# A fused attention and two-mixer kernel on one core: exponentials turned in two by rows for every head pair, and a new instruction order

## The chip, the core and the metric

The kernel runs on one core of a Trainium2 chip. The metric is device time in microseconds (us), the median of three runs. The core's engines work from queues of their own: TensorE (PE in the profile, with PEld for its weight loads), VectorE (DVE), ScalarE (ACT), GpSimd (POOL) and SyncE (SP), which issues most of the transfers.

## What is computed

Three stages one after the other, for batch 4, sequence 448, model width 768:

```python
q_n, k_n = rmsnorm(q, g_q), rmsnorm(k, g_k)            # 12 heads of 64
attn = softmax(scale * q_n @ k_n.T)
x = (attn @ v) put together to [4, 448, 768]
h = relu(x @ w_in); u, v = halves of h                  # "moe", widths 512 and 512
v_n = (v - mean(v)) / sqrt(var(v) + 1e-6)
x = (u * (w_spatial @ v_n + b_spatial)) @ w_out
u = x + (relu(x.T @ w_tok1) @ w_tok2).T                 # "moe2"
out = u + relu(u @ w_ch1) @ w_ch2
```

## The kernel before

**Head pairs.** Attention runs over 24 pairs of heads (`NP`), six for each batch item. A pair's queries are cut into four chunks `c` of T = 112 rows. For a pair, `load` fetches raw q and k, `norms` and `scale` divide the rows by their root mean square (for the first pair `first` does it), and `transposed` turns q and k on TensorE into `qt` and `kt` (called `whole` in the profile for the first eight pairs, `WHOLE = 8`). For each chunk `scores` makes the two heads' 112x448 scores in two PSUM banks, VectorE takes the negated row maximum `nm`, ScalarE writes `e`, the exponentials, and sums them. `turned` turns `e` on TensorE into `et`, in seven blocks of 128 columns, by way of PSUM tiles `tp`; ScalarE or VectorE copies these to SBUF. `values` multiplies `et` by v into `av`, VectorE divides by the sums (`over`), and the result goes on as `xp`.

**Two ways to turn.** For pairs under `HALVED = 8` a chunk is turned by seven transposes of all 112 rows. From pair 8 on each of the seven is done as two, of rows 0 to 63 and of rows 64 to 111, with their own PSUM tiles, issued as one joined group. The copies out of PSUM then take 448 and 336 columns, as they do in the other way.

**Weights and the mixers.** While the pairs run, `prepare_v`, `prepare_uo` and `prepare_next` fetch the mixers' weights, convert them (ScalarE takes the absolute value of a word, VectorE does four integer steps, ScalarE rounds the high part, GpSimd subtracts for the low part; tiles `word`, `wv`, `wpart`) and write some of them back to DRAM. `moe` runs for a batch item once its six pairs are done: `vps`, a normalisation over tokens whose root is made by `rsqrt` (ScalarE Ln and Exp, then Newton steps), `ups`, `sps`, `xps`. After the attention come `h1ps` and `u_ps`, and then two products in Strassen form, `h2ps` and `o_ps`.

**Order.** Nothing is issued as it is written down. Every operation is put into a `Plan` with an estimated cost and its dependencies. `issue` runs a list scheduler (`place`) back and forth, then shifts the weights by a list of random seeds (`NUDGES`), places once more, and emits every engine's queue in the order of the planned starts. So one list sets the order of all engines and of the transfers. `warmers` puts matmuls without a use into planned idle times of TensorE longer than `IDLE` = 1500 ns: one for each `PACE` ns, on the first PSUM bank by number that is free in the gap.

All operations are recorded through one helper, so nearly all rows have line 464, the emitting line of `issue`; the useless matmuls have line 456. Rows are told apart by their tiles.

Of the kernel before, what the change touches and what calls it, by code (L numbers as in the profile page):

```python
# [15 lines left out]
AF = mybir.ActivationFunctionType  # L16
# [136 lines left out]
class Plan:  # L153
# [8 lines left out]
    def add(self, engine, fn, args, kwargs):  # L162
# [6 lines left out]
        if out is None:  # L169
# [6 lines left out]
        op.port = engine == "gpsimd" and bool(sbuf) or engine == "vector" and (  # L176
            len(sbuf) > 1 and free(sbuf[1].shape) > 1
            or len(ins) == len(sbuf) and fn in ("tensor_scalar", "tensor_copy"))

# [208 lines left out]
    def warmers(self, start, bank, closes):  # L388


        ops = self.ops
        busy = {}
        for t, n in bank.items():
            us = [i for i, ts in closes.items() if t in ts]
            first = min(start[i] for i in us)
            last = max(start[i] + ops[i].cost + ops[i].late for i in us) + TO["tensor"]
            busy.setdefault(n, []).append((first, last))
        order = sorted((i for i, op in enumerate(ops) if op.engine == "tensor"), key=lambda i: (start[i], i))
        found = {}
        for a, b in zip(order, order[1:]):  # L400
            end = start[a] + ops[a].cost
            idle = start[b] - end
            if idle < IDLE or end < 10000:
                continue
            for n in range(Banks.ALL):
                if all(last <= end or first >= start[b] for first, last in busy.get(n, ())):
                    break
            else:
                continue
            found[b] = [n] * int((idle - SPARE) / PACE)  # L410
        return found
# [59 lines left out]
SWITCH, NEAR, FAR, EARLY = 300, 2500, 10000, 95000  # L471
NUDGED = 4000
NUDGES = (
# [21 lines left out]
)  # L495
ENGINES = "gpsimd", "scalar", "sync", "tensor", "vector"
IDLE, SPARE, PACE = 1500, 200, 275
SHARED = {"vector": "gpsimd", "gpsimd": "vector"}
# [17 lines left out]
def nudged(weight, seed, engines):  # L516


    h = mixed(seed)
    g = mixed(h)  # L520
    at, reach, size = h % NUDGED, (20, 60, 150, 400)[g & 3], (150, 500, 1500, 4000)[g >> 2 & 3]
    way, who = g >> 4 & 3, ENGINES[(g >> 6) % 5]
    weight = list(weight)
    for i in range(max(0, at - reach), min(len(weight), at + reach)):
        if way in (0, 3) or engines[i] == who:
            u = mixed(seed * 2654435761 + (0 if way & 1 else i) & 0xFFFFFFFF)
            weight[i] += size * ((u >> 8) / 8388608.0 - 1.0)
    return weight
# [33 lines left out]
def attention_moe_mixer(  # L562
# [155 lines left out]
    class Attention:  # L718
# [75 lines left out]
        def first(self):  # L794
# [6 lines left out]
            def squares(a, on):  # L801
                sq = p.tile([T, 2, S], F32, tag="e", bufs=EB, name="e").rearrange("p r s -> p (r s)")
                sq = sq[:, :n * D].rearrange("p (n d) -> p n d", d=D)
                if on is nc.scalar:
                    on.activation(sq, raw[:, a], AF.Square)
                else:
                    on.tensor_tensor(sq, raw[:, a], raw[:, a], op=ALU.mult)
                return sq

            def root(a, on, sq, behind=(), copied=()):  # L810
                ss = p.tile([P, n], F32, tag=f"ss{a}", bufs=1, name="ss")
                ss.tile.after = list(behind)
                nc.vector.reduce_sum(ss[:T], sq, axis=AX.X)
                self.r[0][a] = rsqrt(p, ss[:T], T, n, 1.0 / D, f"r{a}", bufs=1, on=on, wait=copied)
# [21 lines left out]
        def scale(self, i):  # L836
# [4 lines left out]
            if i >= WHOLE:  # L841
# [5 lines left out]
                return  # L847
            for a in range(2) if i else (1,):
                on = nc.gpsimd if i > 1 else nc.vector
# [4 lines left out]
        def transposed(self, i, a, wait=()):  # L854
# [13 lines left out]
            t.tile.after = list(t.tile.after) + list(wait)  # L868
            nc.scalar.activation(t, tpf, AF.Copy, scale=1.0 if a == 0 else self.gg[:, 0:1])
            if a:  # L870
# [138 lines left out]
        def start(self):  # L1009
# [5 lines left out]
            self.gg = self.p.tile([P, 1], F32, tag="gg", bufs=1, name="gg")  # L1015
            nc.vector.tensor_tensor(self.gg, g[:, 0:1], g[:, 1:2], op=ALU.mult)
            nc.vector.tensor_scalar(self.gg, self.gg, float(D) ** -0.5, None, ALU.mult)

# [38 lines left out]
    G = S // R  # L1057
    HALVED = 8
    HALVES = (0, R), (R, T - R)
# [158 lines left out]
    def moe(mp, b):  # L1218
# [20 lines left out]
        for t, m in TOK:  # L1239
# [18 lines left out]
            nc.vector.bn_aggr(mv, bs)  # L1258
            r = rsqrt(mp, mv[:, 1:2], P, 1, 1.0, "lr")
            nc.vector.tensor_scalar(vr, vr, mv[:, 0:1], r, ALU.subtract, ALU.mult)  # L1260
# [416 lines left out]
```

## Time and profile before

| | |
|---|---|
| Median of 3 runs | 848.29 us (847.06 to 849.16) |
| The profiled execution, its own time | 851.01 us |
| Its span, first to last instruction | 849.1 us |
| TensorE busy | 837.8 us (99%) |
| VectorE, ScalarE, GpSimd busy | 675.6 (80%), 527.2 (62%), 344.3 us (41%) |
| Chain of work that ended last | PE 85%, ACT 5%, DMA 4%, DVE 4% |
| Mean granted TensorE clock | 0.996 |

Busy times are sums of records. Matmuls are pipelined, so the record of one overlaps the next: the time that a group takes on TensorE is read from its start to the start of the next group, not from its length. PEclk is the granted clock, 1.00 for 2.4 GHz and 0.50 for 1.2 GHz.

### The profile page before, as it was taken

To read this page: it belongs to the slowest core of one execution; us is meant where nothing else is said; L and a number is where in the kernel's file an instruction comes from. 1 tells how busy PE (TensorE), PEld (TensorE's weight loads), DVE (VectorE), ACT (ScalarE), POOL (GpSimd) and SP (SyncE) were. 2 spreads that over 40 slices of the span, in tenths; PEclk is the share of its full clock that TensorE was granted. 3 is DMA by queue.
4 is the path that set the end of the run, shared out by engine and by line. 5 is a ranking of instruction groups with operands and counts; after the bars stand their busy time and mean duration, and the time that the engine had idled before them with its cause. 6 is when DMAs were issued, how large, how long until landed. Compare 5 with 4: busy or idle time off the path is not lost.

```text
span 849.1 us, 16503 instructions
## 1 busy us (share of the span) xinstructions
PE 837.8 (99%) x5538; PEld 704.6 (83%) x5538; DVE 675.6 (80%) x1340; ACT 527.2 (62%) x1268; POOL 344.3 (41%) x431
## 2 busy tenths in 40 slices
PE   7999999999999999999999999999999999999998
PEld 5555467778678876787799999999999999999998
DVE  5799899886787778877376577988989976998873
ACT  5999899898777778766243465654345654343331
POOL 2457545654445523242143222525331118515460
PEclk9999999999999999999999999999999999999999
DMA  6556676856765767466968787767555645742441
GB/s 158 154 152 167 203 225 177 247 162 176 238 194 147 192 179 209 111 182 188 319 208 260 220 281 239 243 195 215 159 168 173 215 127 158 231 140 78 141 145 66
DMA packets 158532, 157.94 MB, mean 186 GB/s; under 512 B 79216, under 2 KB 141616, under 8 KB 158448
## 3 DMA queue, kind: packets, MB, share of 16 engines
q1 hardware_dynamic: 157984, 156.86, 61.4%
q8 instruction: 44, 0.72, 0.3%
q14 instruction: 40, 0.33, 0.1%
q10 hardware_dynamic: 464, 0.03, 0.0%
HBM read 117.95 MB, written 38.88 MB: 185 GB/s over the span
## 4 chain that ended last, share of the span: by engine, by line
PE 85%; ACT 5%; DMA 4%; DVE 4%; issue 1%; POOL 1%; SPq 1%; ACTq 0%; POOLq 0%; DVEq 0%
PE o_ps L464 18%; PE h2ps L464 18%; PE xps L464 7%; PE ups L464 7%; PE av L464 7%; PE tp L464 6%; PE sc L464 5%; PE vps L464 5%; PE sps L464 4%; PE h1ps L464 4%; PE u_ps L464 3%; ACT e L464 2%; DMA raw<-in_moe_w_in_dram 1%; DVE nm L464 1%; SPq L464 1%
## 5 line engine op out<-in xcount | busy, mean ns | idle before, releaser
L464 PE MATMUL h2ps<-op,w 128*128 128x448 f32 x756 | 154.1, 366 | 0.0
L464 PEld LDWEIGHTS o_ps<-w,op 128*128 128x128 f32 x900 | 154.0, 188 | 0.0
L464 PE MATMUL o_ps<-w,op 128*128 128x384 f32 (+1 forms) x900 | 153.9, 332 | 0.0
L464 PEld LDWEIGHTS h2ps<-op,w 128*128 128x128 f32 x756 | 141.6, 188 | 11.2
L464 ACT ACTIVATE e<-sc,nm 112x448 f32<-112x448 f32 x184 | 120.9, 686 | 4.6 <-DVE nm L464 4.4
L464 DVE TENSOR_REDUCE nm<-sc 112x1 f32<-112x448 f32 x192 | 110.1, 614 | 7.4 <-PE sc L464 6.7
L464 ACT ACTIVATE op<-c 128x768 fp32r<-128x768 f32 x49 | 41.5, 847 | 83.1 <-PE o_ps L464 72.6
L464 POOL TENSOR_TENSOR src<-src 128x384 f32<-128x384 f32 x48 | 61.0, 1281 | 72.9 <-DMA src<-c_d 60.7
L464 PEld LDWEIGHTS tp<-ident,e 64*128 64x128 f32 (+2 forms) x1120 | 56.6, 140 | 26.6 <-ACT e L464 8.5
L464 ACT ACTIVATE et<-tp 128x448 f32<-128x448 f32 (+1 forms) x144 | 72.4, 557 | 5.6 <-PE tp L464 5.2
L464 DVE TENSOR_SCALAR word<-word 128x256 f32<-128x256 f32 (+5 forms) x132 | 61.3, 468 | 16.8 <-ACT word L464 15.7
L464 DVE SCALAR_TENSOR_TENSOR word<-raw,word 128x256 uint32<-128x256 uint32 (+2 forms) x132 | 70.4, 534 | 1.8
L464 POOL TENSOR_TENSOR u<-u,o 128x384 f32<-128x384 f32 x28 | 40.4, 1460 | 68.5 <-ACT o L464 38.8
L464 PE MATMUL tp<-ident,e 48*128 48x48 f32 (+2 forms) x1120 | 66.0, 234 | 0.7 <-ACT e L464 0.5
L464 PE MATMUL ups<-xp,wu 128*128 128x448 f32 x288 | 65.9, 368 | 0.0
L464 DVE TENSOR_TENSOR op<-c,op 128x768 fp32r<-128x768 f32 x49 | 55.5, 1132 | 10.9 <-ACT op L464 10.9
L464 PE MATMUL av<-et,v 128*64 128x448 f32 x288 | 61.1, 550 | 1.3 <-ACT e L464 0.9
L464 PEld LDWEIGHTS ups<-xp,wu 128*128 128x128 f32 x288 | 53.7, 188 | 6.5 <-ACT e L464 0.7
L464 DVE TENSOR_TENSOR c<-c,h2ps 128x448 f32<-128x448 f32 x84 | 49.7, 612 | 9.6 <-PE h2ps L464 9.3
L464 PE MATMUL xps<-wo,g 128*128 128x384 f32 x288 | 55.1, 340 | 0.0
L464 PE MATMUL sc<-kt,qt 64*112 64x448 f32 x384 | 52.9, 384 | 0.4 <-DVE over L464 0.4
L464 PE MATMUL vps<-wv,xp 128*128 128x512 f32 x216 | 52.8, 397 | 0.0
(146 smaller groups left out, 1599.7 us busy)
## 6 DMA issues: line engine op xcount, KB each, us to landing
src<-c_d SPq DMA_DIRECT2D x132, 192.0 KB
wu<-wu_d SPq DMA_DIRECT2D x16, 768.0 KB
wo<-wo_d SPq DMA_DIRECT2D x16, 768.0 KB
raw<-in_moe_w_ch_dram SPq DMA_DIRECT2D x36, 256.0 KB
raw<-in_moe_w_ch_dram SPq DMA_DIRECT2D x24, 384.0 KB
raw<-in_q_dram SPq DMA_DIRECT2D x48, 112.0 KB
over<-over_d SPq DMA_DIRECT2D x48, 112.0 KB
u<-u_d SPq DMA_DIRECT2D x28, 192.0 KB
```

Of the source, the lines that this page charges most:

```text
L464: getattr(getattr(self.nc, op.engine), fn)(*args, **kwargs)
```

## The change

1. `HALVED` is 0 in place of 8: the first eight pairs, too, are turned in two by rows.
2. For the first pair the squares of k (ScalarE) and the row sums of both q and k (VectorE) are done in halves, k's scaling on VectorE in two halves, and the copy of `kt` out of PSUM half on ScalarE and half on VectorE. The product `gg` of the two gains moves from VectorE to GpSimd.
3. In `moe` the root's five small steps (one before Ln, four Newton steps) move from VectorE to GpSimd, for 16 token tiles.
4. `PACE` is 546 in place of 275, and `warmers` takes, of the banks that are free in a gap, the one whose last use ended first.
5. The planner counts other VectorE operations as users of the port that VectorE and GpSimd share; the seeds are all new (319 in place of 228), and they act on the first 3813 operations (4000 before). The order of all queues is therefore another one.

```diff
-            len(sbuf) > 1 and free(sbuf[1].shape) > 1
-            or len(ins) == len(sbuf) and fn in ("tensor_scalar", "tensor_copy"))
+            len(sbuf) > 1 and (fn == "tensor_tensor" or free(sbuf[1].shape) > 1)
+            or len(ins) == len(sbuf) and fn in ("tensor_scalar", "tensor_copy") and free(ins[0].shape) > 1)
...
+            spare = []
             for n in range(Banks.ALL):
                 if all(last <= end or first >= start[b] for first, last in busy.get(n, ())):
-                    break
-            else:
-                continue
-            found[b] = [n] * int((idle - SPARE) / PACE)
+                    spare.append((max([last for _, last in busy.get(n, ()) if last <= end], default=0.0), n))
+            if spare:
+                found[b] = [min(spare)[1]] * int((idle - SPARE) / PACE)
...
-NUDGED = 4000
+NUDGED = 3813
...
-IDLE, SPARE, PACE = 1500, 200, 275
+IDLE, SPARE, PACE = 1500, 200, 546
...
-    for i in range(max(0, at - reach), min(len(weight), at + reach)):
+    for i in range(max(0, at - reach), min(NUDGED, at + reach)):
...
-                    on.activation(sq, raw[:, a], AF.Square)
+                    for h in (slice(0, C), slice(C, n)):
+                        on.activation(sq[:, h], raw[:, a, h], AF.Square)
...
-                nc.vector.reduce_sum(ss[:T], sq, axis=AX.X)
+                for h in (slice(0, C), slice(C, n)):
+                    nc.vector.reduce_sum(ss[:T, h], sq[:, h], axis=AX.X)
...
-            for a in range(2) if i else (1,):
+            if not i:
+                roots = self.r[0][1][:T]
+                for c in range(0, C, 2):
+                    raw = self.raw[0][:, 1, c:c + 2].rearrange("p c r d -> p (c r) d")
+                    nc.vector.tensor_tensor(
+                        raw, raw, roots[:, 2 * c:2 * c + 4].unsqueeze(2).to_broadcast([T, 4, D]), op=ALU.mult)
+                return
+            for a in range(2):
...
-            nc.scalar.activation(t, tpf, AF.Copy, scale=1.0 if a == 0 else self.gg[:, 0:1])
+            if a and not i:
+                n = S // 2
+                nc.scalar.activation(t[:, :n], tpf[:, :n], AF.Copy, scale=self.gg[:, 0:1])
+                nc.vector.tensor_scalar(t[:, n:], tpf[:, n:], self.gg[:, 0:1], None, ALU.mult)
+            else:
+                nc.scalar.activation(t, tpf, AF.Copy, scale=1.0 if a == 0 else self.gg[:, 0:1])
...
-            nc.vector.tensor_tensor(self.gg, g[:, 0:1], g[:, 1:2], op=ALU.mult)
-            nc.vector.tensor_scalar(self.gg, self.gg, float(D) ** -0.5, None, ALU.mult)
+            nc.gpsimd.tensor_tensor(self.gg, g[:, 0:1], g[:, 1:2], op=ALU.mult)
+            nc.gpsimd.tensor_scalar(self.gg, self.gg, float(D) ** -0.5, None, ALU.mult)
...
-    HALVED = 8
+    HALVED = 0
...
-            r = rsqrt(mp, mv[:, 1:2], P, 1, 1.0, "lr")
+            r = rsqrt(mp, mv[:, 1:2], P, 1, 1.0, "lr", on=nc.gpsimd)
```

## Rows read from the trace of the kernel before

**Rows 1.** Windows by stage: stretch, its length, busy of each engine (instructions), PEclk, DMA.
```profile
20.00:30.00 10.00, 9.91 (x62) 7.70 (x63) 6.50 (x14) 7.70 (x22) 3.67 (x7) 0.80 0.61 172
30.00:97.00 67.00, 64.43 (x387) 33.07 (x386) 61.07 (x144) 66.13 (x190) 39.76 (x63) 1.00 0.63 169
97.00:120.00 23.00, 22.52 (x137) 14.34 (x134) 19.59 (x54) 18.64 (x52) 12.68 (x18) 1.00 0.65 186
120.00:541.00 421.00, 420.31 (x3243) 344.10 (x3242) 320.97 (x737) 290.74 (x758) 171.45 (x236) 1.00 0.69 209
```

**Rows 2.** Waits of TensorE, 120 to 545: total us, times, longest.
```profile
PE sc L464 <- DVE over L464: 0.4, 1, 0.4
```

**Rows 3.** Timeline of TensorE, 9 to 30 us: start, length, instruction.
```profile
10.77 3.27 PE L464 MATMUL sc<-whole 64*112 64x448 f32 x16 [0.72 <-ACT whole L464]
15.09 5.54 PE L456 MATMUL warm<-ident 128*128 128x128 f32 x16 [1.05 <-ACT e L464]
20.42 1.70 PE L464 MATMUL tp<-ident,raw 112*128 112x112 f32 x8
21.91 3.24 PE L464 MATMUL tp<-ident,e 112*128 112x112 f32 x21
25.08 1.76 PE L464 MATMUL sc<-whole 64*112 64x448 f32 x8
```

**Rows 4.** Windows of 1 us around the first idle time.
```profile
17.00:18.00 1.00, 0.94 (x4) 0.52 (x3) 1.00 (x3) 1.00 (x2) 0.90 (x2) 0.63 0.45 101
...
24.00:25.00 1.00, 1.00 (x11) 0.94 (x10) 0.39 (x1) 0.66 (x4) 0.00 (x0) 0.96 0.54 115
```

**Rows 5.** Windows of 10 us: the head at its loosest.
```profile
80.00:90.00 10.00, 8.82 (x57) 4.53 (x53) 9.11 (x22) 9.41 (x28) 8.71 (x15) 1.00 0.80 236
```

**Rows 6.** Timeline of TensorE, 30 to 60 us: full-height transposes.
```profile
42.52 1.50 PE L464 MATMUL tp<-ident,e 112*128 112x112 f32 x14
43.96 0.97 PE L464 MATMUL av<-et,v 128*64 128x448 f32 x4
...
45.80 0.89 PE L464 MATMUL tp<-ident,e 112*128 112x112 f32 x7
46.62 2.17 PE L464 MATMUL sc<-whole 64*112 64x448 f32 x8
```

**Rows 7.** Timeline of TensorE, 305 to 345 us: transposes in two by rows.
```profile
305.48 1.02 PE L464 MATMUL tp<-ident,e 64*128 64x64 f32 x28
306.32 0.85 PE L464 MATMUL sc<-kt,qt 64*112 64x448 f32 x6
```

**Rows 8.** Windows, instructions on tile wpart alone (busy and count by engine).
```profile
30.00:80.00 50.00, 7.05 (x19) 5.81 (x10) 3.03 (x4) 1.00 0.60 157
80.00:97.00 17.00, 5.84 (x13) 2.48 (x6) 2.18 (x3) 1.00 0.71 206
```

**Rows 9.** Timeline of ScalarE, 58 to 72 us: conversion steps.
```profile
71.08 0.71 ACT L464 ACTIVATE wpart<-raw 128x256 f32<-128x256 f32 x1
71.42 0.68 ACT L464 ACTIVATE wpart<-wpart 128x256 fp32r<-128x256 f32 x1
```

**Rows 10.** Timeline of all engines, 0 to 34 us: start, length, engine, instruction.
```profile
7.13 0.16 DVE L464 TENSOR_TENSOR gg<-g 128x1 f32<-128x1 f32 x1 [0.37 <-DMA g<-in_g_k_dram]
...
11.51 0.20 POOL L464 TENSOR_TENSOR r0z<-r0y 112x8 f32<-112x8 f32 x1 [1.24 <-ACT r0y L464]
...
12.37 0.20 POOL L464 TENSOR_TENSOR r0y<-r0y,r0z 112x8 f32<-112x8 f32 x1
...
12.75 0.66 ACT L464 ACTIVATE word<-raw 128x512 f32<-128x512 f32 x1 [1.32 <-DMA raw<-in_moe_w_in_dram]
...
16.65 1.27 DVE L464 TENSOR_TENSOR raw<-raw,ry 112x512 f32<-112x512 f32 x2
```

**Rows 11.** Timeline of VectorE, 410 to 440 us: one token tile's root.
```profile
417.35 0.16 DVE L464 TENSOR_TENSOR lrz<-lry 128x1 f32<-128x1 f32 x1 [0.50 <-ACT lry L464]
...
418.12 0.55 DVE L464 TENSOR_SCALAR vr<-vr,mv,lry 128x512 f32<-128x512 f32 x1
```

50 rows, old and new, of the table NUDGES are left out of this document.

## The prediction

> **What bounds the kernel now.** I read the windows by stage first, then TensorE's waits, then the timelines of the head. From 120 us on TensorE is the bound and has no slack: 420.31 of 421 us busy [rows 1], and in that whole stretch one wait of 0.4 us [rows 2]. Behind 541 us come the two Strassen products, which the change leaves alone apart from their order. So an edit pays only if it takes work off TensorE or lets TensorE begin its unbroken run earlier; microseconds taken from VectorE or GpSimd after 120 us are worth nothing by themselves.
>
> The head, up to 120 us, is different: two engines are full at once. Between 30 and 97 us ScalarE is busy 66.13 of 67 us and TensorE 64.43, VectorE 61.07 [rows 1]. From 97 us, when the first six pairs are through and `vps` of the first batch item gives TensorE something else to do, ScalarE has room again (18.64 of 23) and TensorE is still full (22.52). Before 30 us there is a hole: TensorE ends the first scores at 14.04, waits, runs 16 useless matmuls from 15.09 to 20.42, and turns pair 1 only then [rows 3]. The clock falls to half in those matmuls (0.63 in the window at 17 us) and is back in the window at 24 us [rows 4]. ScalarE loses 2.30 us between 20 and 30 us to this [rows 1].
>
> **The change part by part.**
>
> *Turning in two by rows.* Now seven transposes of 112 rows take from 42.52 to 43.96 for two chunks, 0.72 us each, and 0.82 us for one that is followed by scores (45.80 to 46.62) [rows 6]. In the later pairs two chunks done in two by rows take 305.48 to 306.32, 0.42 us each [rows 7]: twice the instructions, but the two row groups run together. The first eight pairs have 32 chunks; each gives back 0.30 to 0.40 us, together 9.6 to 12.8 us of TensorE. I take 0.35, so 11.2: 8.4 in the 24 chunks of the first six pairs, 2.8 in the last two pairs. The copies out of PSUM keep their two sizes, so ScalarE and VectorE gain nothing. Each chunk now needs both `tp` banks at once; the later pairs live with that in a stretch where TensorE doesn't wait [rows 1, 2], and I charge nothing for it. If they had to wait for a bank, it would be behind one copy on ScalarE, and the cost is inside the cover worked out below.
>
> *Fewer useless matmuls.* 16 of them at one per 275 ns stand for a planned gap of 4.6 to 4.88 us; at one per 546 ns the same gap holds 8. They took 5.33 us for 16 [rows 3], 0.33 each, so 8 take 2.7. Pair 1 is scaled at 16.65 + 1.27 = 17.92 [rows 10]. The last useless matmul would end at 17.8 if they began at 15.09, earlier with a bank that is free sooner; TensorE then turns pair 1 at about 17.9 and not at 20.42, 2.5 us earlier. What ScalarE can make of it is its idle time there, 2.3. If the new order puts the exponentials of another chunk into the gap, the planned gap itself is different; the bounds are 0 and 2.5, and I take 2.0. A half-clock stretch may remain: it costs the 21 transposes from 21.91 to 25.08 0.151 us each [rows 3] against 0.103 to 0.117 [rows 6], some 0.9 us that the order before pays as well.
>
> *The first pair in halves.* `gg` held VectorE for 0.37 us [rows 10], waiting for its gains; on GpSimd it stands ahead of the query's root steps, which begin only at 11.51 with the row shown [rows 10], so it delays nothing. Halving a square, a sum, a scaling and a copy lets the next engine start about 0.2 us earlier four times. That is up to 1.3 us at the first scores (10.77). The exponentials behind them can't use all of it: ScalarE stands 1.32 us ahead of a weight conversion at 12.75 that waits for a transfer, and the query's root ends with the step at 12.37 [rows 10]. Nothing here moves that transfer except the order. Bounds 0 and 1.3, nearest row the conversion: 0.5.
>
> *Newton steps on GpSimd.* Four steps on VectorE take 417.35 to 418.12, 0.77 us [rows 11]. On GpSimd the first pair's steps show the pace: from the start of the first to that of the fourth 0.86 us (11.51 to 12.37), 0.29 each [rows 10], so four take 1.15, 0.4 us more, and a step can stand behind another GpSimd operation. The waiting `vr` holds VectorE's queue, and `vn` and the first `sps` come after it. What hides it is `ups`, which TensorE runs until then, and VectorE's idle time (320.97 of 421 busy [rows 1]). Without that cover 16 tiles cost 16 x 0.4 = 6.4 us. The relief on VectorE, 16 x 0.77 = 12 us, is worth nothing where TensorE is the bound. I take 0, bounds 6.4 lost and, as VectorE is free more often before a row maximum, 1 gained.
>
> *Port, seeds, order.* These change no amount of work. They decide how much of TensorE's saving becomes time; that is the next part.
>
> **The cover.** In the first six pairs TensorE would be ahead by 0.5 + 2.0 + 8.4 = 10.9 us. ScalarE must follow. It can give its idle time, 2.3 us between 20 and 30 and 0.9 between 30 and 97 [rows 1], and it can put off the conversions for `prepare_uo`: 10 + 6 operations on `wpart` in that stretch [rows 8], one start every 0.34 us (71.08 to 71.42) [rows 9], 16 x 0.34 = 5.4 us, for which it has 130 us of room between 120 and 541 (290.74 of 421). Together 8.6. So ScalarE stops the first six pairs 2.3 us short of what TensorE could do. The last two pairs run beside `vps` and give their 2.8 in full: 8.6 + 2.8 = 11.4. The order before leaves TensorE 3.05 us idle between 30 and 120 (2.57 + 0.48) [rows 1] with both engines full; with the slack more uneven I expect half as much again, 1.5 us. Sum: 9.9, **10 us less**.
>
> The Trainium skill, page TensorEngine Tiling (Array Packing), section Performance Considerations, warns against just this: tiling speeds up TensorE but not the emptying of PSUM, which may become the bottleneck. The full ScalarE of rows 1 agrees. By that rule alone, with nothing put off, the sum would be the second rival's.
>
> The profiled execution took 851.0 us, its span 849.1. Ten less is 841 for an execution like it. The median of the runs shown is 848.29, 2.7 below the profiled one, and the prediction is on that scale: **838.3 us**.
>
> **The rivals.**
>
> *ScalarE is no limit.* The new order also puts off other conversions, and every microsecond off TensorE counts: 0.5 to 1.3, 2.5, and 11.2 to 12.8, 14.2 to 16.6 in all, so 832 to 834. For it: the order before got both engines to over 96% between 30 and 97. Against: `wv` must be ready for `vps`, and six pairs need every exponential.
>
> *ScalarE is the limit and nothing is put off.* Then the first six pairs give only its idle time, 2.3 + 0.9, and the last two 2.8: 6.0 at most, 2.8 if the hole before 30 us stays. 842.3 to 845.5. For it: ScalarE is full for 67 us [rows 1]. Against: 16 operations there aren't needed until `ups`.
>
> *TensorE gets gaps and loses its clock.* This ends on the other side. With less work in a stretch that ScalarE paces, TensorE idles more often between 30 and 97 us. The one fall in the trace came after the idle time at 14.04 to 15.09 and lasted from 17 to 24 us [rows 3, 4]; seven microseconds at half rate cost up to 3.5. Three such falls eat the 10 us; from four on the kernel is slower, at 852 with four. For it: the head would have some 10% idle. Against: between 80 and 90 us TensorE is busy 8.82 of 10 and the clock stays 1.00 [rows 5].
>
> *It comes out even.* The new order meets a transfer or a late `vn` after 120 us where TensorE has no slack, and gives 6 to 10 us back (the 6.4 of the Newton steps would do with the second rival). 846 to 850.
>
> **How the numbers follow.** Forecast (7 to 13 us less) 0.45; ScalarE no limit (over 13) 0.16; ScalarE the limit (2.5 to 7) 0.18; even 0.09; slower 0.12. About 0.3%, 2.5 us, is what a measurement of this kernel can tell from no change. Faster by more than that 0.79, within it 0.09, slower 0.12. The range takes the forecast, the first rival down to 831.5, and nearly all of the second up to 845.5: some 0.79.
>
> **What the profile after would show.** Transposes of `e` in 64 and 48 rows alone, some 0.42 us a chunk also in the first pairs: the saving on TensorE is right. About eight useless matmuls and pair 1 turned near 18 us. The first `vps` near 89 us in place of 98, and all later stages moved by the same 9 to 11 us with TensorE still without waits: the cover is right. ScalarE full and TensorE with gaps until 95 us or so: the second rival. PEclk under 0.9 in windows between 30 and 97 us: the third. Waits of `sps` or `vr` for GpSimd's `lry` after 120 us: the Newton steps cost. I would be wrong if the stretch from 120 us grew, since I took it as fixed.

## The result, and the profile after

The changed kernel took 853.86 us (median of 6 runs, 852.33 to 854.3), the kernel before 848.41 beside it: ratio 1.0059, 95% interval 1.0046 to 1.0073. It is 0.6% slower, where I forecast 10 us less. Its profiled execution took 854.23 us, its span 852.4.

The windows by stage after, which answer to [rows 1]; below them two of 1 us from the head:

```profile
20.00:30.00 10.00, 9.37 (x90) 6.05 (x92) 7.99 (x15) 8.88 (x26) 4.20 (x9) 0.83 0.52 144
30.00:97.00 67.00, 61.09 (x548) 29.95 (x550) 61.89 (x146) 65.94 (x192) 35.90 (x57) 1.00 0.60 168
97.00:120.00 23.00, 22.95 (x175) 15.04 (x172) 18.89 (x48) 18.32 (x52) 14.67 (x24) 1.00 0.58 163
120.00:541.00 421.00, 416.64 (x3212) 340.07 (x3211) 309.85 (x663) 288.08 (x754) 192.32 (x315) 1.00 0.71 210
...
13.00:14.00 1.00, 1.00 (x4) 0.45 (x4) 0.83 (x2) 0.89 (x4) 0.48 (x3) 0.50 1.24 246
23.00:24.00 1.00, 1.00 (x6) 0.45 (x4) 0.55 (x1) 1.00 (x4) 0.00 (x0) 0.50 0.28 63
```

Between 30 and 97 us TensorE is busy 61.09 us in place of 64.43 [rows 1], while ScalarE is as full as before (65.94 against 66.13). The stretch that I took as fixed now holds idle time: 416.64 of 421, against 420.31 [rows 1]. TensorE is at half clock twice ahead of 30 us. TensorE's waits from 120 to 545 us, where [rows 2] had one line of 0.4:

```profile
PE tp L464 <- DVE et L464: 1.2, 1, 1.2
PE sps L464 <- ACT vn L464: 0.9, 1, 0.9
PE xps L464 <- DMA wo<-wo_d: 0.8, 1, 0.8
PE tp L464 <- ACT e L464: 0.7, 2, 0.3
PE sc L464 <- ACT e L464: 0.4, 1, 0.4
```

TensorE's timeline at the start, beside [rows 3], and around 93 us:

```profile
12.69 4.65 PE L464 MATMUL sc<-whole 64*112 64x448 f32 x16 [3.00 <-DVE whole L464]
17.26 1.58 PE L456 MATMUL warm<-ident 128*128 128x128 f32 x6
20.06 0.96 PE L464 MATMUL tp<-ident,raw 112*128 112x112 f32 x8 [1.21 <-issue]
20.94 1.08 PE L464 MATMUL tp<-ident,e 64*128 64x64 f32 x28
22.27 2.56 PE L464 MATMUL sc<-whole 64*112 64x448 f32 x6 [0.25 <-ACT whole L464]
...
93.61 1.04 PE L464 MATMUL tp<-ident,e 64*128 64x64 f32 x14
94.58 0.97 PE L464 MATMUL av<-et,v 128*64 128x448 f32 x4
95.48 1.22 PE L464 MATMUL tp<-ident,e 64*128 64x64 f32 x28
96.63 0.97 PE L464 MATMUL av<-et,v 128*64 128x448 f32 x4
```

The first scores start at 12.69 and not 10.77, and take 4.65 us in place of 3.27, the first 2.8 us of it at half clock. Pair 1 is turned at 20.06. A chunk in halves takes 0.97 us at 93.61 (start to start of `av`) and 0.58 at 95.48, not the 0.42 that I expected from [rows 7]. The row at 93.61 counts as one group, but in the trace its second transpose starts 0.41 us behind its first. The first `vps` starts at 101.19 (98.19 in the trace shown of before).

The first scores are late because of a transfer. ScalarE's timeline there: `sq` of pair 1 stands ahead of the copy `whole` that the first scores need, and waits 2.83 us for pair 1's q, whose fetch stands behind pair 1's k in the DMA queue.

```profile
10.92 0.63 ACT L464 ACTIVATE sq<-raw 112x512 f32<-112x512 f32 x1 [2.83 <-DMA raw<-in_q_dram]
11.46 0.43 ACT L464 ACTIVATE whole<-tp,gg 128x224 f32<-128x224 f32 x1
```

### The profile page after: what moved, and what is told of

The parts are those of the page before. It is cut to its first block, busy times and chain, and to the rows that moved or that the text cites. A ratio compares the mean times of both kernels' runs of the same rounds, so it can differ in the third digit from the quotient of the medians.

```text
span 852.4 us, 16930 instructions
## 1 busy us (share of the span) xinstructions
PE 831.6 (98%) x5752; PEld 697.3 (82%) x5752; DVE 666.4 (78%) x1262; ACT 526.3 (62%) x1269; POOL 360.9 (42%) x513
## 4 chain that ended last, share of the span: by engine, by line
PE 77%; ACT 8%; DMA 6%; DVE 4%; POOL 2%; issue 2%; SPq 1%; ACTq 0%; DVEq 0%; POOLq 0%
PE o_ps L464 18%; PE h2ps L464 18%; PE xps L464 7%; PE ups L464 6%; PE tp L464 5%; PE sc L464 4%; PE av L464 4%; PE vps L464 4%; PE sps L464 4%; PE u_ps L464 4%; PE h1ps L464 4%; ACT e L464 3%; SPq L464 1%; ACT et L464 1%; DVE nm L464 1%
## 5 line engine op out<-in xcount | busy, mean ns | idle before, releaser
L464 PEld LDWEIGHTS h2ps<-op,w 128*128 128x128 f32 x756 | 141.8, 188 | 11.2
L464 POOL TENSOR_TENSOR src<-src 128x384 f32<-128x384 f32 x48 | 56.3, 1181 | 81.3 <-DMA src<-c_d 73.8
L464 PEld LDWEIGHTS tp<-ident,e 64*128 64x128 f32 (+1 forms) x1344 | 51.7, 139 | 34.1 <-ACT e L464 18.3
L464 DVE TENSOR_TENSOR op<-c,op 128x768 fp32r<-128x768 f32 x49 | 56.8, 1159 | 10.2 <-ACT op L464 10.2
L464 PE MATMUL tp<-ident,e 48*128 48x48 f32 (+1 forms) x1344 | 60.1, 226 | 2.3 <-ACT e L464 1.4
L464 PEld LDWEIGHTS xps<-wo,g 128*128 128x128 f32 x288 | 49.9, 188 | 3.8 <-issue 1.7
```

The source lines that it names most:

```text
L464: getattr(getattr(self.nc, op.engine), fn)(*args, **kwargs)
```

## The experiments

My theory after the result: ScalarE sets the pace of the first six pairs, the order puts nothing off, and TensorE's saving turns into waiting. The rivals: the halves save nothing; the Newton steps cost; the late start costs; TensorE's clock costs. Unless said otherwise a run has the changed kernel's order, planned as there, and only what is emitted differs; `op.swap` is what is emitted in place of an instruction, and `...` in an edit marks left-out lines. The runs were timed in several sessions, each with the kernel before beside it, so ratios are the safer comparison between two runs.

**The halves of the first eight pairs undone**

```diff
+                    if i < 8:
...
+                            turning.swap.append(("tensor", "transpose", (
+                                flat[:, (n - n0) * T:(n - n0 + 1) * T], e[:, at0:at0 + P], ident[:T, :T]), {}))
```

> The changed kernel with every queue in the same order, and one thing undone: the first eight pairs are turned by seven transposes of 112 rows, emitted at the place of the joined group of fourteen, into the same two PSUM banks; the copies keep their sizes (448 and 336 columns). Theory A (ScalarE paces the first six pairs, so TensorE's saved time is idle time there): 853.9 plus 0 to 4 us, the part that is not idle time being that of the last two pairs (2.8 us at most); TensorE's idle time before the first vps falls. Theory B (the halves save their 9.6 to 12.8 us and the new order gives more than that away elsewhere): 862 to 867 us.

854.33 us, ratio to before 1.0059 (1.0038 to 1.0079): the changed kernel's time. In this order the halves of the first eight pairs give nothing that can be told from the noise (some 2 us either way).

**The Newton steps back on VectorE**

```diff
+        if tag == "lr":
+            for op in nc.ops[first_op:]:
+                if op.engine != "scalar":
+                    op.swap = [("vector", *op.call)]
```

> The changed kernel, same order of emission, with the five small steps of the mixer's root back on VectorE. If the Newton steps on GpSimd are what stalls TensorE after 120 us (the chain runs over them and the waiting subtraction near 346 and between 428 and 434 us): 1 to 4 us faster, 850 to 853. If those stalls belong to the order: within 1 us of 853.9, or slower, since VectorE's queue then holds 80 operations more.

855.03 us, ratio 1.0065 (1.0042 to 1.0087). Taking the steps at nothing was right.

**Pair 1's q fetched ahead of its k**

```diff
+        q = [i for i in loads if self.second[self.ops[i]] == "q"]
+        seq = [i for i in seq if i not in q]
+        at = seq.index(next(i for i in loads if self.second[self.ops[i]] == "k"))
+        return seq[:at] + q + seq[at:]
...
-        for i in sorted(range(len(ops)), key=lambda i: (start[i], i)):
+        for i in self.sequence(start):
```

> The changed kernel, with one move in the transfer queue: the second pair's q is fetched ahead of its k, as the kernel before does. In the changed kernel the square of that q stands ahead of the copies of the first pair's k on ScalarE, and waits for the transfer until 10.92 us; the first scores begin at 12.69 in place of 10.77. If the first six pairs are paced by ScalarE from its first exponential on, a start 2 us earlier moves everything: 851 to 852.5. If the late start is swallowed by later idle time: 853.9 within 1 us.

852.85 us, ratio 1.0045 (1.0023 to 1.0067), about 1 us less, within the runs' spread. The first scores start at 11.01, but that isn't the edit's doing: in ten other profiles with the order's own fetches they start between 10.60 and 11.39 (full height 11.01, second profile of the changed kernel 11.06). The 12.69 belongs to one execution.

**ScalarE's absolute values left out**

```diff
             nc.scalar.activation(a.bitcast(F32), high.bitcast(F32), AF.Abs)
+            nc.ops[-1].swap = []
             nc.vector.tensor_scalar(a.bitcast(F32), a.bitcast(F32), least, most, ALU.max, ALU.min)
+            nc.ops[-1].swap = [("vector", "tensor_scalar", (
+                a.bitcast(F32), high.bitcast(F32), -most, most, ALU.max, ALU.min), {})]
```

> The changed kernel, same order, without ScalarE's absolute value in each weight conversion; VectorE's first step reads the raw high word and clamps it from below and above by the largest float (it leaves out the flush of magnitudes below the smallest normal float, which the drawn weights don't have; the sign is shifted out behind it in any case). This takes 6 operations of 0.58 us and 9 of 0.33, 6.5 us, off ScalarE ahead of the first vps, and adds nothing in number to VectorE. Theory A (ScalarE paces): 4 to 6.5 us faster, 847 to 850, and TensorE's idle time before vps shrinks by as much. Theory B (the order, not ScalarE): within 1.5 us of 853.9. VectorE, at 84.5 of 101 us, could take ScalarE's place if the strided read is slower: then 1 to 3 us faster.

847.75 us, ratio 0.9988 (0.9967 to 1.0009), 6 us under the changed kernel, with the first `vps` at 97.69, 3.5 us earlier. Every weight conversion loses one of its ScalarE steps and keeps all its others. By the time this is theory A, but its other sign didn't come: TensorE's gaps ahead of the first `vps` are 10.1 us, against 11.6 and 9.6 in the two profiles of the changed kernel. The edit also makes each conversion one step shorter, so that its result is ready sooner, and no run tells this from ScalarE's relief. ScalarE as the pace is thus well supported, not shown alone.

**The same with the halves undone, and in the order before**

> The changed kernel's order with both edits: no absolute value on ScalarE, and the first eight pairs turned in full height again. With ScalarE relieved by 6.5 us ahead of the first vps, the transposes in two by rows should begin to count if TensorE is the next limit. Theory A (ScalarE still paces the first six pairs): 847.8 plus 0 to 3 us. If TensorE is the limit once ScalarE has 6 us less to do: 853 to 857, the halves' gain coming back in full.

850.26 us, ratio 1.0010 (0.9994 to 1.0027): with ScalarE relieved the halves are worth some 2 us, 2.5 by the medians and 1.9 by the ratios, whose intervals just overlap.

> The kernel before, its own order, without the absolute value on ScalarE (the same edit as in the changed kernel). If ScalarE paces the first six pairs in this order too: 4 to 6 us faster, 842 to 845, with the first vps near 93 us in place of 98. If TensorE, with its transposes in full height, is as much the limit there: 0 to 2 us faster, 846 to 848.

845.7 us, ratio 0.9965 (0.995 to 0.9981): the order before gains as well, about 3 us, half of what the new one gains, and between the two cases of the expectation. Its first `vps` is at 94.81, against 98.19 and 95.22 in the two profiles of the kernel before, so little of this gain is to be seen there.

> The changed kernel's order with both repairs: no absolute value on ScalarE, and the second pair's q fetched ahead of its k. If both act on ScalarE's pace they add: 847.8 less 1 to 2 us, 846 to 847. If the start is swallowed: 847.8 within 0.7 us.

848.55 us, ratio 0.9987 (0.9971 to 1.0003): nothing beyond the absolute values. It was timed beside the run with the halves undone (850.26) and is 1.7 us under it, which bears out the 2 us above.

**Fewer useless matmuls in the order before**

```diff
-IDLE, SPARE, PACE = 1500, 200, 275
+IDLE, SPARE, PACE = 1500, 200, 546
```

> The kernel before, its own order, with one useless matmul for each 546 ns of planned idle time in place of 275: four in place of eight in the one gap that has any. TensorE should turn the second pair near 18 us in place of 20.42. By the prediction's term 2.0 us faster (0 to 2.5): 846.3. If ScalarE paces and its idle time between 20 and 30 us (2.3 us) shrinks, the same. If the clock falls for longer with half of the matmuls gone: 848.3 or slower.

848.23 us, ratio 0.9989 (0.9976 to 1.0002): some 1 us, not told from nothing. Pair 1 is turned at 17.19, against 20.42 and 18.94 in the two profiles of the kernel before, so the earlier turning came and little of it became time.

**The halves undone where TensorE is the bound**

The edit is shown against the run that undid the first eight pairs' halves:

```diff
-                    if i < 8:
+                    if i >= 8:
```

> The changed kernel's order, with pairs 8 to 23 turned in full height and the first eight in halves: the reverse of the run that undid the halves of the first eight pairs. 64 chunks take seven transposes of 112 rows in place of fourteen of 64 and 48. Theory A (halves save TensorE 0.30 to 0.40 us a chunk, and this becomes time where TensorE is the bound): 19 to 26 us above the changed kernel, 873 to 880 us. Rival B (halves are worth next to nothing wherever they stand, because two row groups don't run together as well as I read): within 3 us of the changed kernel, 851 to 857 us. Rival C (half of it): TensorE's waits in the later pairs take up some of it, 860 to 868 us.

867.1 us, ratio 1.0214 (1.0196 to 1.0233): 13.2 us above the changed kernel's 853.86, for 64 chunks 0.21 us each. By its number this is rival C, but the waits explain little of it: TensorE's idle time from 120 to 541 us only falls from 4.4 to 3.0 us (busy 418.05 of 421). The halves are worth time, but at 0.21 us a chunk (0.23 with the 1.4 us of idle time), not at the 0.35 that I took. A chunk in full height takes 0.66 us here, less than the 0.72 and 0.82 of [rows 6]:

```profile
305.60 0.89 PE L468 MATMUL tp<-ident,e 112*128 112x112 f32 x7
306.26 0.60 PE L468 MATMUL xps<-wo,g 128*128 128x384 f32 x2
```

Others take longer (0.76 us at 313.18), so this explains a part of the difference at most.

**The conversions put off by hand**

```diff
+            if 40000 <= t < 185000:
+                when[number[op]] = t + (185000 - t) * 0.4
```

The milder runs have 0.2 and 0.1 in place of 0.4.

> The changed kernel's order, with the weight conversions for the expert matrices (prepare_uo) that stand between 40 and 185 us emitted later: the one planned for 40 us goes to 98, those behind it follow with a shift that shrinks to nothing at 185; the loads of the converted matrices follow where they must. This does by hand what my prediction took the new order to do by itself. Theory A (ScalarE paces the first six pairs, and conversions put off give it the 5.4 us I counted): the first vps 3 to 5 us earlier than in the changed kernel, at 96 to 98 us, and 2 to 4 us off the whole, 850 to 852 us. Rival B (the exponentials wait for something else, the roots and copies on VectorE and GpSimd): the first vps within 1 us of 101 and the whole at 853 to 855 us. Rival C: the conversions meet ups and xps late, first vps earlier but the gain lost behind it, 853 to 857 us.

> put_off and no_abs together; as in no_abs, the flush of magnitudes under the smallest normal number is left out of the weight conversions. Theory A (ScalarE still paces the first six pairs without the absolute values): 2 to 3 us below no_abs, 844.5 to 846 us. Rival B (without the absolute values TensorE or VectorE paces the head): within 1 us of no_abs, 847 to 849 us.

878.58 us, ratio 1.0353 (1.0333 to 1.0373), and 873.32, ratio 1.029 (1.0271 to 1.0309). The instructions on `wpart` ahead of the first `vps` (columns VectorE, ScalarE, GpSimd), first in the changed kernel, then with the shift:

```profile
30.00:80.00 50.00, 6.84 (x20) 4.80 (x8) 2.92 (x4) 1.00 0.58 161
80.00:101.00 21.00, 5.49 (x15) 3.87 (x8) 2.20 (x3) 1.00 0.63 178
```

```profile
30.00:80.00 50.00, 1.37 (x4) 0.00 (x0) 0.00 (x0) 1.00 0.45 117
80.00:97.00 17.00, 0.00 (x0) 0.00 (x0) 0.00 (x0) 1.00 0.32 79
```

The 16 ScalarE steps of those windows are gone, and the first `vps` starts at 97.13, 4.06 us earlier: the first half of theory A. With them went 31 of the 35 VectorE steps and all 7 of GpSimd, so this run doesn't show that it was ScalarE's relief. Behind the first `vps` much more is lost, and both times are above every case of the expectations. TensorE's windows with the shift, and the waits of the DMA queue's engine from 95 to 200 us (total, times, longest):

```profile
120.00:140.00 20.00, 15.14 (x98) 9.97 (x94) 14.06 (x34) 12.16 (x39) 11.70 (x23) 0.83 0.83 233
140.00:200.00 60.00, 48.31 (x355) 34.62 (x355) 46.58 (x107) 42.76 (x118) 33.22 (x53) 0.88 0.61 177
```

```profile
SPq L479 <- DVE wpart L479: 13.4, 11, 3.9
SPq L479 <- POOL wpart L479: 7.1, 5, 3.1
SPq L479 <- DMA wu_d<-wpart: 6.0, 4, 2.9
```

One queue issues the loads of raw weights, the stores of converted ones and their loads back, and it stands behind conversions that come late. In the changed kernel the first two of these waits are 7.0 and 5.5 us. TensorE also stands at half clock for some 27 us between 120 and 207 us in this execution. So a milder shift:

> As the run that put off the conversions for the expert matrices, with half the shift: the one planned for 40 us goes to 69, one planned for 85 us to 105, shrinking to nothing at 185. About four of the nine pieces ahead of the first vps come behind it. Theory A (ScalarE's queue ahead of the first vps decides, and the loss behind it in the stronger shift came from bunched transfers): first vps at 98.5 to 100 us and 1 to 3 us off the changed kernel's time, 851 to 853 us. Rival B (any putting off runs into the transfers of wu and wo): first vps earlier, but the whole at 855 us or more.

> The same with a quarter of the first shift: the conversion planned for 40 us goes to 54.5, one planned for 95 us to 104; about two of the nine pieces come behind the first vps. Theory A: first vps at 99.5 to 100.5 us, 0.5 to 1.5 us off the changed kernel's time, 852.5 to 853.5 us. Rival B: 854 us or more.

871.53 us, ratio 1.0265 (1.0248 to 1.0282), and 871.17, ratio 1.0258 (1.0233 to 1.0282). Rival B, and worse than it said: even the quarter shift costs 17 us, and there the first `vps` is later (104.89; 100.51 with half the shift). Moving conversions alone past the other instructions of these queues isn't to be had; the order as a whole would have to be found for it.

**Both kernels profiled again**

> The kernel before once more, unchanged, for a second profile: the one shown is of an execution 2.7 us above the median. Theory A (a usual execution of the kernel before has its first vps 2 to 3 us earlier than the shown 98.19, as the run with fewer useless matmuls had at 95.41, so that the whole loss of 5.5 us lies ahead of the first vps): first vps at 95 to 96.5 us. Rival B (the shown head is the usual one, and the shown execution lost its 2.7 us elsewhere): 97.7 to 98.7 us, and some 2.5 us of the loss lie behind the first vps.

> The changed kernel once more, unchanged, for a second profile. Theory A (its head is as late in every execution): first scores at 12.4 to 12.9 and first vps at 100.5 to 102 us. Rival B (the shown execution had a slow start): first scores near 11 and first vps under 100 us.

847.79 and 857.21 us. The second profile of before, windows by stage:

```profile
20.00:30.00 10.00, 9.69 (x72) 6.35 (x70) 9.47 (x21) 10.00 (x30) 3.49 (x7) 1.00 0.61 149
30.00:97.00 67.00, 64.62 (x381) 33.31 (x379) 60.65 (x140) 64.81 (x187) 40.65 (x64) 1.00 0.62 170
97.00:120.00 23.00, 21.72 (x133) 14.27 (x132) 19.69 (x57) 18.91 (x55) 11.50 (x17) 1.00 0.73 209
```

The clock never falls, ScalarE is busy 10.00 of 10 us between 20 and 30 (7.70 in [rows 1]), and the first `vps` starts at 95.22. The half clock of [rows 4] doesn't belong to every execution: of the 104 of the kernel before on record, 25 have a mean granted clock of 0.996 or less, as the shown one has, and 42 one of 1.000. The hole of 2.3 us on which my cover rested is not in this execution, and against it the changed kernel is 6.0 us late at the first `vps`: by its number theory A. But the first `vps` isn't the same point in the two orders. Ahead of it the new order has 120 records of scores in place of 112, 28 chunks turned in place of 26.6, and 14 more transposes of other tiles. Two of these groups, in the changed kernel's trace, with the `vps` that follows:

```profile
98.76 1.72 PE L464 MATMUL sc<-whole 64*112 64x448 f32 x8
100.54 0.72 PE L464 MATMUL tp<-ident,raw 64*128 64x64 f32 x14
101.19 3.05 PE L464 MATMUL vps<-wv,xp 128*128 128x512 f32 x12
```

By these starts some 3 of the 6.0 us are work moved ahead. That the whole loss lies ahead of the first `vps` is thus not shown. The first `h2ps`, behind which both kernels do the same, is the sounder mark: 541.37 against 534.99. The second profile of the changed kernel has its first scores at 11.06 and the first `vps` at 104.09, so neither of the two cases. From 56 us, where it is 1.2 us ahead of the first profile, to the first `vps` it loses 4.1 us. Some of its 1-us windows:

```profile
63.00:64.00 1.00, 0.66 (x14) 0.51 (x13) 1.00 (x3) 1.00 (x6) 0.50 (x1) 1.00 0.78 237
64.00:65.00 1.00, 0.12 (x2) 0.12 (x4) 0.77 (x3) 1.00 (x5) 1.00 (x2) 0.80 0.58 140
66.00:67.00 1.00, 1.00 (x10) 0.44 (x10) 0.98 (x4) 1.00 (x5) 0.05 (x1) 0.50 1.03 261
...
91.00:92.00 1.00, 0.73 (x5) 0.14 (x1) 1.00 (x3) 1.00 (x4) 1.00 (x2) 0.96 0.57 148
93.00:94.00 1.00, 1.00 (x7) 0.67 (x7) 1.00 (x2) 1.00 (x4) 1.00 (x1) 0.50 0.12 29
```

TensorE goes idle around 64 and 89 to 92 us, falls to half clock, and stays there to 71 and nearly 99 us. ScalarE is busy all along.

**TensorE kept busy in the gaps**

```diff
-IDLE, SPARE, PACE = 1500, 200, 546
+IDLE, SPARE, PACE = 1500, 200, 275
+MORE = {10676: 8, 61892: 3, 85161: 4, 87294: 3}
```

`MORE` gives the number of useless matmuls ahead of the matmul or transpose of that planned start (the entry 61892 put in none); the second run has 5 in place of 8 and fetches pair 1's q ahead of its k. The old `PACE` gives 7 in place of 3 ahead of pair 1.

> The changed kernel's order with more useless matmuls where TensorE stands idle in the head: 8 ahead of the first scores, 7 in place of 3 ahead of pair 1's transposes (the kernel before's pace), 4 and 3 ahead of the two groups of transposes of raw rows near 89 and 92 us. Two profiles of the changed kernel have TensorE at half clock for 6.8 and 20 us ahead of 120 us, each time behind idle time of this kind; a second profile of the kernel before has none. Theory A (the half-clock stretches make up a good part of the 5.5 us): the granted clock stays at 1.00 ahead of 120 us but for one stretch at most, first vps at 98 to 100 us, whole 849.5 to 852 us. Rival B (ScalarE paces the head, and a slow TensorE only waits less): clock as in A, but first vps at 100.5 to 102 and whole 853 to 855 us. Rival C (the useless matmuls hold the first scores and the transposes up): 855 us or more.

> The same, with pair 1's query rows fetched ahead of its key rows and 5 useless matmuls ahead of the first scores. Theory A (start and clock together): first scores near 11, first vps at 96.5 to 99 us, whole 848.5 to 851 us, so that what is left of the loss against the kernel before is ScalarE's 9 further instructions. Rival B: first vps at 100 us or later and whole 852 to 854 us, as the earlier fetch alone gave 852.85.

861.38 us, ratio 1.0137 (1.011 to 1.0163), and 859.37, ratio 1.0118 (1.0089 to 1.0147). The first is rival C, the second slower than either of its cases. The first of them on TensorE:

```profile
89.08 2.13 PE L461 MATMUL warm<-ident 128*128 128x128 f32 x8 [1.73 <-ACT e L469]
...
93.89 2.37 PE L461 MATMUL warm<-ident 128*128 128x128 f32 x6
...
107.28 3.03 PE L469 MATMUL vps<-wv,xp 128*128 128x512 f32 x12
```

The useless matmuls near 89 us waited themselves, by the profile for an exponential on ScalarE (which reads, I take it, the bank that they write), pushed the work behind them back, and the clock fell after all (0.72 in the mean from 89 to 107 us). Ahead of 89 us the first run has no half clock. Its first scores, behind their useless matmuls, start at 13.85, 1.2 us later than in the changed kernel, and those at 68.96 there start at 68.14, 0.8 us earlier. So 2.0 us are gained in between, where the changed kernel loses 3.4 us to half clock: TensorE's clock is worth something there, but not all of what it loses.

**The best version: the order before without the absolute values, and fewer useless matmuls**

> The kernel before with the absolute values left out of the weight conversions (and with them the flush of magnitudes under the smallest normal number) and one useless matmul for each 546 ns of planned idle time, 4 in place of 8. If the two gains measured alone (3.4 and 0.8 us) add up: 844 to 845 us. If the useless matmuls were noise: 845.5 to 846 us.

844.88 us, ratio 0.9962 (0.9948 to 0.9977). It is under both kernels; against the run without the absolute values alone (0.9965) the useless matmuls can't be told from nothing.

## Why the prediction was wrong, step by step

**The cover is the first step that failed.** I let ScalarE follow TensorE for 8.6 us, of which 5.4 were to come from 16 conversion steps that "it can put off", and 2.3 from its idle time between 20 and 30 us. The new order put nothing off: ScalarE has 17 steps on `wpart` ahead of the first `vps` (15 in both profiles of before) and 251 instructions in all (242 and 240). That work could wait is no evidence that a planner lets it wait. By hand the same steps gave 4.06 us at the first `vps`, but VectorE's and GpSimd's steps went with them, and the same move cost some 29 us behind it. And the idle time of 2.3 us belonged to a start that about a quarter of the executions have, by their clock. That ScalarE sets the limit is supported by the times: the conversions without their absolute values gave 6 us in this order and 3 in the other, while the halves of the first eight pairs gave nothing with ScalarE full and some 2 us with ScalarE relieved. That the conversions also became a step shorter is a rival that no run excludes. The Trainium skill, page TensorEngine Tiling (Array Packing), section Performance Considerations, warns that tiling doesn't speed up the emptying of PSUM. The traces agree in so far as the halves gave nothing where ScalarE was full, and became time for the later pairs; but of the 251 instructions 114 make the exponentials and their sums and 42 copy turned chunks, and no run tested those copies by themselves.

**The term of 1.5 us for gaps is the second step that failed, and it turned the sign.** Without any cover the sum still gave 2.8 to 6.0 us less, as the second rival had it: nothing was put off, as it said, but it held that the rest stays as it was. It didn't: the new order leaves TensorE idle more. I summed the gaps over 0.1 us between TensorE's records from 8 us to the first `h2ps`, behind which both kernels do the same (one execution each):

| | gaps | lost to half clock | first `h2ps` |
|---|---|---|---|
| before | 6.2 | 3.4 | 537.98 |
| before, second profile | 7.0 | 0 | 534.99 |
| changed, halves undone | 13.1 | 3.4 | 542.37 |
| changed | 15.7 | 3.4 | 541.37 |
| changed, second profile | 14.4 | 10.2 | 544.38 |
| changed, no absolute values | 13.8 | 1.7 | 535.77 |

(Lost to half clock: half the time at half clock, ahead of 120 us.) With the halves undone the changed kernel has 6.1 us of gaps and 3.4 of half clock more than the second profile of before, and saves 5 useless matmuls of 0.53 us (three took 1.58): 6.9, against 7.4 measured. Against the first profile of before it is 6.9 of gaps, the same clock and the same saving: 4.3, against 4.4 measured. The halves then take 32 x 0.21 = 6.7 us of work off and add 2.6 of gaps; only 1.0 of the difference shows at the first `h2ps`, so some 3.1 us more must be waits that leave no gap between records. That last step is argued from the sum. The halves undone, the Newton steps and the start leave the order as the cause of the gaps by exclusion; the first pair's halves were not undone by themselves.

**The clock goes with nearly half of the loss.** The 23 executions of the kernel before with a mean granted clock of 0.996 took 850.95 us in the median, the 42 at 1.000 took 847.8. The changed kernel's six have 0.994 to 0.996, and the five at 0.996 took 854.01. So at the same clock the changed kernel is 3 us slower, and the rest of its 5.5 us goes with the clock, which falls more often in the new order. The falls follow gaps, so this doesn't show which of the two costs the time.

**Halves: right in sign, mis-sized.** 0.35 us a chunk, from two places in the timeline; 0.21 as measured over 64 chunks. By that measure the 11.2 us were 6.7, if a chunk of the first pairs is worth as much as a later one. Why the timeline's two places show more than the whole gives stays open.

**The useless matmuls: misread.** The 16 records of [rows 3] are 8 matmuls, each with two records. The planned gap was therefore about half of the 4.6 to 4.88 us that I worked out; the changed kernel has 3, not 8. The term of 2.0 measured about 1, with an interval from nothing to 2.0.

**The start: nothing.** I gave it 0.5. The first scores start at 10.77 and 10.93 in the two profiles of before, and in all but one with the new order, and no useless matmuls put ahead of them, between 10.60 and 11.39. Even the late start of the trace shown doesn't last: near 69 us (68.96 against 68.83 in the second profile of before) both kernels start the same scores by number, with as many of `av` behind them.

**The Newton steps: right.** Nothing that the run could tell, in either direction.

**From 120 us on: wrong, as I said it could be.** I took it as fixed, apart from a gain of 2.8 in the last two pairs; its idle time grew by 3.7 us, in waits of 0.4 to 1.2 us. From the first `vps` to the first `h2ps` the changed kernel takes 440.18 us, against 439.78 and 439.77 in the two profiles of before, although some 3 us of work had moved ahead of that stretch and two of its pairs are turned in halves. This is the mechanism of "it comes out even", joined to that of ScalarE as the limit.

**The rival on the other side was half right.** TensorE did get gaps and lose its clock: 3.4 us' worth in one profile, 10.2 in the other. Of the 3.4 ahead of 30 us some 2 become time by the run with more useless matmuls, and between the two profiles of before, where one has no fall, 3.0 us lie at the first `h2ps`. The later two falls, in the second profile, cost up to the 4.1 us that it lost. The four falls that the rival asked for are reached in neither profile: the clock is a part of the loss, not the whole.

What stays open: why the order leaves these gaps between 69 us and the first `vps`. In the second profile of before the chain of waits holds no transfer between 60 us and the first `vps`. In the changed kernel's it does:

```profile
79.27 2.52 DMA over<-over_d
...
89.00 2.90 DMA over_d<-rows
...
92.59 2.80 DMA over<-over_d
...
98.61 1.88 POOL raw L464 x2
...
101.26 2.75 PE vps L464 x11
```

Three transfers of 8.2 us in all stand in it, and a scaling on GpSimd that the transposes ahead of `vps` wait for. No run took them out, so they are not shown to be the cause; in the run without absolute values, 6 us faster, two of them (2.87 and 2.94 us) and the scaling stand in the chain as well. The halves alone in the order before weren't tried either.

## What to carry to other kernels

When two engines are full in the same stretch, work taken off one of them is worth what the other can give up, and that must be found in the order itself (count its instructions ahead of the next stage), not in what could wait. A searched order is a change of its own: it can take more, in gaps of half a microsecond all over, than the edit that it comes with gives. Before a hole in a profile is counted as a reserve, look whether a second execution has it. And two orders are compared at a point behind which the same work remains: the first instruction of a stage can stand later because more of the other work was done ahead of it.

## What the runs showed of the hardware

The half-clock stretches ahead of 120 us differ between executions of one kernel: none or 6.8 us in the two profiles of the kernel before, 6.8 or some 20 us in those of the changed one. They follow idle time of TensorE of 1 to 3 us, but not every such gap brings one: near 65 us the two profiles of the changed kernel have gaps of 1.07 and 1.08 us, and only the second falls; the first run with more useless matmuls has one of 1.08 us there and no fall either. A useless matmul of f32 leaves two records (4 and 3 put in near 89 and 94 us left 8 and 6), a transpose of f32 one (a chunk in halves, 14 transposes, leaves 14). In the changed kernel's profile the record of a transpose of `e` in halves is 0.22 us long in the median, while two of them start every 0.06 us; a wait that is shorter than such a record can leave no gap, so TensorE's busy share hides part of its waiting.
